# Transposes of q, k and the attention output on the DMA crossbar in place of TensorE

## The chip, the cores and the metric

The kernel runs on one core of one Trainium2 chip. The metric is the device time of one execution in microseconds; several runs are taken, and their median counts. The kernel before has a median of 389.23 us over 3 runs (389.01 to 389.64). Beside the timed runs there is one profiled execution, from which all views of the profile come.

## The reference

The work is a causal attention with a forget gate, followed by a two-layer network with an exact GELU. There are 8 batches of 8 heads, 576 tokens and 64 dimensions a head; the network sees 4608 tokens of 512 values, 2048 in the middle.

```
scores = q @ k.T / sqrt(64) + (cum[q] - cum[k])      # cum = cumsum(log(clip(f, 1e-4, 1)))
scores = where(key > query, -1e9, scores)
attn   = softmax(scores) ; o = attn @ v              # per batch and head
x      = o, heads side by side                       # 4608 x 512
out    = gelu(x @ w_in) @ w_out                      # 4608 x 2048, 4608 x 512
```

Inputs and output are float32; the kernel multiplies in bfloat16.

## The kernel before, in words

All order is written out by hand: each engine runs its instructions in the order of the program text, and only data and buffers make it wait. SP issues loads of f and v and all stores, POOL the loads of q, k and the weights (they are cast to bfloat16 on the way).

**Attention of a batch.** Two heads make a pair, and a batch has four pairs. `scores(b, i, t)` makes the tile t (0 to 3) of key-by-query scores of pair i for both heads: 2 or 4 matmuls (L251) into one of two score buffers, an exp on ScalarE (L261), and a causal mask on POOL (L263). `attend(b, i, h, ms)` (L282) multiplies the masked exps by the weighted v, with a column for the row sums; `normalize` (L295, L296, VectorE) divides, which gives the pair's x tile of tokens by (head, dimension). The program attends to a pair while the next pair's scores are made.

**The transposes.** The scores need q and k with the 64 dimensions on partitions: `qA[i]` holds the first head of the pair in the upper half and zeros in the lower, `qB[i]` the reverse, `kT[i]` both heads of k. q and k arrive as tiles of 96 partitions, six tokens in each. `transposes_pe(b, i)` transposes pair i with twelve TensorE transposes against an identity (L209); each takes two neighbouring tokens' 64 dimensions, so that even tokens lie in the upper and odd ones in the lower 64 partitions, and eight VectorE copies (L221) put them in their columns. The network needs x with features on partitions: `to_xT(b, i)` makes five transposes (L306) and one VectorE copy (L309) into `xT_sb`.

**The network.** A chunk is 512 tokens. `gemm1(c, ffb)` makes one of 16 blocks of the middle layer: four matmuls (L318), one for each pair's features, and a GELU on ScalarE (L330). `gemm2(c)` is a generator that gives one matmul (L350) at a time, 64 in a chunk; every sixteenth ends an output tile, which VectorE copies (L359) and SP stores (L360). Both use the two buffers of `m_psum`.

**How they interleave.** Batch 0 has a routine of its own, and its transposes stay as they are. For each later batch b, `attention(b, ...)` runs the attention, and after each `scores` call takes some matmuls from `gemm2(b - 1)`; the table FILL (FILL_1 for batch 1) says how many: a row for each pair, a column for each tile, and a last row for the places behind the last pair's scores. Then come the 16 blocks of `gemm1(b)`, and between them the transposes of the next batch's q and k, and POOL's weighing of its v. The first matmul of a block needs x of pair 0, the last x of pair 3. After batch 7 the remaining chunk follows without attention.

Of the kernel before, what the change touches and what calls it, by code (L numbers as in the profile page):

```python
# [9 lines left out]
BF16 = mybir.dt.bfloat16  # L10
# [4 lines left out]
P = 128  # L15
S = 576
D = 64
H = 8
HP = 4
# [3 lines left out]
JT = 6  # L23
PT = 96
# [25 lines left out]
def kernel(  # L50
# [10 lines left out]
    nc = tc.nc  # L61
    B = q.shape[0]
# [13 lines left out]
    qk_pool = ctx.enter_context(tc.tile_pool(name="qk", bufs=1))  # L76
    v_pool = ctx.enter_context(tc.tile_pool(name="v", bufs=1))
    e_pool = ctx.enter_context(tc.tile_pool(name="e", bufs=3))
    x_pool = ctx.enter_context(tc.tile_pool(name="x", bufs=3))
    g_pool = ctx.enter_context(tc.tile_pool(name="g", bufs=2))  # L80
    o_pool = ctx.enter_context(tc.tile_pool(name="outs", bufs=4))
# [5 lines left out]
    qk_of, v_of = {}, {}  # L87

    def load_qk_tokens(b, h0=0, h1=H):

        if b not in qk_of:
            qk_of[b] = [
                qk_pool.tile([PT, H, JT * D], BF16, tag=n, name=f"{n}{b}")
                for n in "qk"
            ]
        for src, dst in zip((q, k), qk_of[b]):
            nc.gpsimd.dma_start(  # L97
                dst[:, h0:h1, :],
                src[b, h0:h1].rearrange("h (p j) d -> p h (j d)", j=JT),
            )  # L100
# [28 lines left out]
    qA = [consts.tile([P, S], BF16, name=f"qA{i}") for i in range(HP)]  # L129
    qB = [consts.tile([P, S], BF16, name=f"qB{i}") for i in range(HP)]  # L130
    kT = [consts.tile([P, S], BF16, name=f"kT{i}") for i in range(HP)]
# [14 lines left out]
    def load_w_out():  # L146
        for kt in range(0, n_ff, 4):
            nc.gpsimd.dma_start(w_out_sb[:, kt : kt + 4, :], w_out_r[:, kt : kt + 4, :])
# [16 lines left out]
    xT_sb = consts.tile([P, n_dm, N_tok], BF16)  # L165
# [27 lines left out]
    def transposes_pe(b, i, in_s=True):  # L193

        shape = [P, 2, JT // 2, PT]
        if in_s:
            both = s_psum.tile([P, 2, 2 * 512], BF16, tag="s", name="s_t")
            pss = [
                both[:, w, 0:S].rearrange("p (h j t) -> p h j t", h=2, j=JT // 2)
                for w in range(2)  # L200
            ]
        else:
            pss = [
                o_psum.tile(shape, BF16, tag="o", name="ps_t") for _ in range(2)
            ]
        for src, ps in zip(qk_of[b], pss):
            for h in range(2):
                for j in range(JT // 2):
                    nc.tensor.transpose(  # L209
                        ps[:, h, j, :],  # L210
                        src[:, 2 * i + h, 2 * j * D : 2 * (j + 1) * D],
                        ident_bf[:PT, :PT],
                    )
        for which, ps in enumerate(pss):
            for h in range(2):
                dst = (qA[i], qB[i])[h] if which == 0 else kT[i]
                rows = dst[h * D : (h + 1) * D, :].rearrange(
                    "d (p j two) -> d two p j", j=JT // 2, two=2
                )
                for odd in range(2):  # L220
                    nc.vector.tensor_copy(  # L221
                        rows[:, odd],
                        ps[odd * D : (odd + 1) * D, h].rearrange("d j p -> d p j"),
                    )

    vw_of = {}

    def weigh_v(b, i, eng=None):
# [17 lines left out]
    def scores(b, i, t):  # L246
        st = s_psum.tile([P, 2, 512], FP32, tag="s", name=f"s{t}")
        c = 0
        for n, q0, w in STILES[t]:
            for h, qt in enumerate((qA[i], qB[i])):  # L250
                nc.tensor.matmul(  # L251
                    st[:, h, c : c + w],
                    kT[i][:, K0[n] : K0[n] + P],
                    qt[:, q0 : q0 + w],
                    start=True,
                    stop=True,
                )
            c += w
        et = e_pool.tile([P, 2, 512], BF16, tag=f"e{t}", name=f"e{t}")
        e_of[b, i, t] = et  # L260
        nc.scalar.activation(et[:, :, 0:c], st[:, :, 0:c], Act.Exp, scale=scale)  # L261
        for c0 in SDIAG[t]:
            nc.gpsimd.affine_select(  # L263
                out=et[:, :, c0 : c0 + P],
                in_=et[:, :, c0 : c0 + P],
                compare_op=Alu.is_ge,
                fill=0.0,
                base=0,
                pattern=[[0, 2], [1, P]],
                channel_multiplier=-1,  # L270
            )

    o_of, x_of = {}, {}

    def attend(b, i, h, ms):
        if (b, i, h) not in o_of:
            o_of[b, i, h] = o_psum.tile([P, NBLK, D + 1], FP32, tag="o", name="o")
        o = o_of[b, i, h]
        for m in ms:
            for n in range(m + 1):  # L280
                t, c = where(n, m)
                nc.tensor.matmul(  # L282
                    o[:, m, :],
                    e_of[b, i, t][:, h, c : c + P],
                    vw_of[b][:, 2 * i + h, n, :],
                    start=(n == 0),
                    stop=(n == m),
                )

    def normalize(b, i, h):  # L290
        if (b, i) not in x_of:
            x_of[b, i] = x_pool.tile([P, NBLK, 2, D], BF16, tag="x", name="x")
        o = o_of[b, i, h]
        r = x_pool.tile([P, NBLK], FP32, tag="r", name="r")
        nc.vector.reciprocal(r, o[:, :, D])  # L295
        nc.vector.tensor_tensor(  # L296
            x_of[b, i][:, :, h, :],
            o[:, :, 0:D],
            r.unsqueeze(2).to_broadcast([P, NBLK, D]),
            Alu.mult,  # L300
        )

    def to_xT(b, i, pool=o_psum, tag="o"):
        ps = pool.tile([P, S], BF16, tag=tag, name="ps_x")
        for m in (4, 3, 2, 1, 0):
            nc.tensor.transpose(  # L306
                ps[:, K0[m] : K0[m] + P], x_of[b, i][:, m, :, :], ident_bf
            )
        nc.vector.tensor_copy(xT_sb[:, i, b * S : (b + 1) * S], ps)  # L309


    g_of = {}
# [50 lines left out]
    def take(gen, n):  # L363
        for _ in range(n):
            if next(gen, "end") == "end":
                return


    def first_attention():
# [37 lines left out]
        scores(0, 2, 3)  # L407
        weigh_v(0, 3)
        to_xT(0, 0, m_psum, "m")
        scores(0, 3, 0)  # L410
        scores(0, 3, 1)
# [10 lines left out]

    FILL = [[5, 7, 4, 4], [2, 3, 3, 2], [2, 3, 3, 2], [2, 2, 2, 2], [8, 4, 4, 0]]
    FILL_1 = [[0, 0, 0, 0], [2, 2, 2, 2], [2, 2, 2, 2], [2, 2, 2, 2], [8, 4, 4, 0]]

    def attention(b, fill, counts):
        for i in range(HP):
            for t in range(4):  # L430
                scores(b, i, t)
                if i >= 2 and t == 0:
                    to_xT(b, i - 2)
                if i and t == 1:
                    attend(b, i - 1, 0, (0, 1, 2))
                elif i and t == 2:
                    attend(b, i - 1, 0, (3, 4))
                    normalize(b, i - 1, 0)
                elif i and t == 3:
                    attend(b, i - 1, 1, (0, 1, 2, 3, 4))  # L440
                    normalize(b, i - 1, 1)
                if b == 1 and i == 0 and t == 2:
                    transposes_pe(1, 3, in_s=False)
                    load_qk_tokens(2)
                take(fill, counts[i][t])
        i = HP - 1
        take(fill, counts[HP][0])
        attend(b, i, 0, (0, 1, 2, 3, 4))
        normalize(b, i, 0)
        to_xT(b, i - 1)  # L450
        take(fill, counts[HP][1])
        attend(b, i, 1, (0, 1, 2, 3, 4))
        normalize(b, i, 1)
        take(fill, counts[HP][2])
        to_xT(b, i)
        take(fill, 999)

    for b in range(B):
        if b == 0:
            first_attention()  # L460
            load_v(1, 0, 4)
            load_v(1, 4, 8)
        else:
            load_v(b + 1)
            attention(b, gemm2(b - 1, b == 1), FILL_1 if b == 1 else FILL)
        for ffb in range(n_ff):
            gemm1(b, ffb)
            if b + 1 < B:
                at = (10, 13, 15) if b == 0 else (0, 4, 8, 11)
                if ffb in at:  # L470
                    transposes_pe(b + 1, at.index(ffb))
                if ffb % 4 == 2:
                    weigh_v(b + 1, ffb // 4)
                if b == 0 and ffb == 2:
                    load_w_out()
        if 0 < b < B - 2:
            load_qk_tokens(b + 2)
# [35 lines left out]
```

## Time and profile before

| | |
|---|---|
| median of 3 runs | 389.23 us (389.01 to 389.64) |
| profiled execution | 389.12 us |
| its span, first to last instruction | 387.2 us |
| mean granted TensorE clock | 0.991 |
| TensorE matmuls busy | 363.6 us, 94% of the span |
| VectorE busy | 204.0 us, 53% |
| ScalarE busy | 217.8 us, 56% |
| GpSimd busy | 130.9 us, 34% |
| moved by DMA | 34.18 MB, mean 88 GB/s |

In the profile's rows PE is TensorE's matmuls, PEld its weight loads, DVE VectorE, ACT ScalarE, POOL GpSimd and SP SyncE; SPq is SP's queue of issues. L12 is line 12 of the kernel. A row of a group ends with its count, busy time, mean duration in ns, and the idle time of the engine before it with what ended that. A row of the chain of waits has a start, a length and what ran. Matmuls are pipelined and their ends are modelled, so a busy TensorE need not be at its peak; the chain counts each piece of its time once.

### The profile page before, as it was taken

To read this page: it belongs to the slowest core of one execution; us is meant where nothing else is said; L and a number is where in the kernel's file an instruction comes from. 1 tells how busy PE (TensorE), PEld (TensorE's weight loads), DVE (VectorE), ACT (ScalarE), POOL (GpSimd) and SP (SyncE) were. 2 spreads that over 40 slices of the span, in tenths; PEclk is the share of its full clock that TensorE was granted. 3 is DMA by queue.
4 is the path that set the end of the run, shared out by engine and by line. 5 is a ranking of instruction groups with operands and counts; after the bars stand their busy time and mean duration, and the time that the engine had idled before them with its cause. 6 is when DMAs were issued, how large, how long until landed. Compare 5 with 4: busy or idle time off the path is not lost.

```text
span 387.2 us, 7532 instructions
## 1 busy us (share of the span) xinstructions
PE 363.6 (94%) x3040; PEld 205.7 (53%) x3093; DVE 204.0 (53%) x448; ACT 217.8 (56%) x293; POOL 130.9 (34%) x261
## 2 busy tenths in 40 slices
PE   2889949999999999999999999999999999999996
PEld 1555536645565546654665556555655465444442
DVE  6483585549346953587358925693469545002011
ACT  4665656425873677457764678358736774621610
POOL 6675715341245134332425144513450242000000
PEclk9999978999999999999999999999999999999999
DMA  7999999145801781068213850188010010002002
GB/s 106 188 195 181 215 208 137 56 111 83 147 29 56 138 122 56 30 139 125 59 47 91 125 99 29 61 138 143 30 54 2 15 42 30 25 29 81 0 29 81
DMA packets 63954, 34.18 MB, mean 88 GB/s; under 512 B 42864, under 2 KB 59248, under 8 KB 63920
## 3 DMA queue, kind: packets, MB, share of 16 engines
q0 software_dynamic: 16896, 13.63, 23.7%
q1 hardware_dynamic: 47024, 20.08, 20.7%
q8 instruction: 24, 0.39, 0.4%
q14 instruction: 10, 0.08, 0.1%
HBM read 37.90 MB, written 9.44 MB: 122 GB/s over the span
## 4 chain that ended last, share of the span: by engine, by line
PE 90%; DVE 5%; ACT 2%; issue 1%; DMA 1%; ACTq 0%
PE ps L350 32%; PE ps L318 31%; PE s L251 13%; PE o L282 7%; PE s_t L209 3%; PE ps_x L306 2%; DVE ot L359 1%; ACT e L261 1%; PE ps_f L174 1%; DVE x L296 1%; DVE xT_sb L309 1%; DMA f_sb<-in_f_dram 1%; DVE kT L221 0%; DVE cum L161 0%; ACT L261 0%
## 5 line engine op out<-in xcount | busy, mean ns | idle before, releaser
L330 ACT ACTIVATE g<-ps 128x512 bf16<-128x512 f32 x144 | 86.0, 597 | 107.7 <-PE ps L318 107.7
L350 PE MATMUL ps<-w_out_sb,g 128*128 128x512 bf16 x540 | 138.9, 380 | 1.7
L318 PE MATMUL ps<-xT_sb,w_in_sb 128*128 128x512 bf16 x559 | 130.0, 379 | 1.5
L261 ACT ACTIVATE e<-s 128x1024 bf16<-128x1024 f32 (+2 forms) x128 | 107.3, 863 | 38.2 <-PE s L251 33.8
L263 POOL TENSOR_SCALAR_AFFINE_SELECT e<-e 128x256 bf16<-128x256 bf16 x160 | 63.8, 413 | 116.6 <-ACT e L261 115.6
L318 PEld LDWEIGHTS <-w_in_sb 128*128 128x128 bf16 x576 | 54.5, 98 | 60.8 <-issue 0.8
L350 PEld LDWEIGHTS <-g 128*128 128x128 bf16 x576 | 50.2, 98 | 40.0
L359 DVE COPY ot<-ps 128x512 f32<-128x512 f32 x36 | 24.8, 690 | 76.5 <-PE ps L350 72.9
L251 PE MATMUL s<-qA,kT 128*128 128x384 bf16 (+2 forms) x192 | 55.9, 299 | 8.5 <-ACT e L261 4.3
L251 PEld LDWEIGHTS <-kT 128*128 128x128 bf16 x384 | 37.7, 102 | 45.5 <-issue 8.2
L221 DVE COPY kT<-s_t 64x288 bf16<-64x288 bf16 x108 | 51.8, 480 | 1.5
L251 PE MATMUL s<-qB,kT 128*128 128x384 bf16 (+2 forms) x192 | 51.5, 300 | 0.3 <-DVE qB L182 0.3
L236 POOL TENSOR_TENSOR vw<-v,wT 128x640 bf16<-128x640 f32 x30 | 38.4, 1280 | 27.0 <-PE o L282 22.3
L295 DVE RECIPROCAL r<-o 128x5 f32<-128x5 f32 x64 | 12.4, 194 | 63.4 <-PE o L282 63.4
L282 PEld LDWEIGHTS <-e 128*128 128x128 bf16 x960 | 40.6, 98 | 8.1 <-DVE x L296 1.3
L282 PE MATMUL o<-vw,e 128*128 128x65 bf16 x960 | 43.9, 194 | 0.1
L221 DVE COPY qA<-s_t 64x288 bf16<-64x288 bf16 x54 | 25.9, 479 | 16.3 <-PE s_t L209 15.3
L296 DVE TENSOR_TENSOR x<-o,r 128x320 bf16<-128x320 f32 x64 | 31.5, 492 | 2.2
L221 DVE COPY qB<-s_t 64x288 bf16<-64x288 bf16 x54 | 25.9, 480 | 0.7
L97 POOL DMA_DIRECT2D q<-in_q_dram x12 | 9.1, 756 | 47.7 <-PE s_t L209 46.5
L309 DVE COPY xT_sb<-ps_x 128x576 bf16<-128x576 bf16 x32 | 14.5, 452 | 8.4 <-PE ps_x L306 8.4
L306 PE MATMUL ps_x<-ident_bf,x 128*128 128x128 bf16 x160 | 14.4, 220 | 2.1 <-DVE x L296 2.1
(49 smaller groups left out, 134.9 us busy)
## 6 DMA issues: line engine op xcount, KB each, us to landing
out_dram<-ot SPq DMA_DIRECT2D x36, 256.0 KB, 2.0
v<-in_v_dram SPq DMA_DIRECT2D x30, 256.0 KB, 4.7
q<-in_q_dram POOLq DMA_DIRECT2D x6, 576.0 KB, 6.3
k<-in_k_dram POOLq DMA_DIRECT2D x6, 576.0 KB, 8.3
v<-in_v_dram SPq DMA_DIRECT2D x20, 128.0 KB, 6.8
w_in_sb<-in_moe_w_in_dram POOLq DMA_DIRECT2D x4, 512.0 KB, 10.3
w_out_sb<-in_moe_w_out_dram POOLq DMA_DIRECT2D x4, 512.0 KB, 10.6
q<-in_q_dram POOLq DMA_DIRECT2D x4, 144.0 KB, 4.2
```

What stands on the lines that cost most here:

```text
L221: nc.vector.tensor_copy(rows[:, odd], ps[odd * D : (odd + 1) * D, h].rearrange("d j p -> d p j"),)
L236: eng.tensor_tensor(vw_of[b][:, hs, :, 0:D], v_of[b][:, hs, :, :], w.unsqueeze(3).to_broadcast([P, 2, NBLK, D]), Alu.mult,)
L251: nc.tensor.matmul(st[:, h, c : c + w], kT[i][:, K0[n] : K0[n] + P], qt[:, q0 : q0 + w], start=True, stop=True,)
L261: nc.scalar.activation(et[:, :, 0:c], st[:, :, 0:c], Act.Exp, scale=scale)
L263: nc.gpsimd.affine_select(out=et[:, :, c0 : c0 + P], in_=et[:, :, c0 : c0 + P], compare_op=Alu.is_ge, fill=0.0, base=0, pattern=[[0, 2], [ ...
L282: nc.tensor.matmul(o[:, m, :], e_of[b, i, t][:, h, c : c + P], vw_of[b][:, 2 * i + h, n, :], start=(n == 0), stop=(n == m),)
L296: nc.vector.tensor_tensor(x_of[b, i][:, :, h, :], o[:, :, 0:D], r.unsqueeze(2).to_broadcast([P, NBLK, D]), Alu.mult,)
L306: nc.tensor.transpose(ps[:, K0[m] : K0[m] + P], x_of[b, i][:, m, :, :], ident_bf)
L318: nc.tensor.matmul(ps, w_in_sb[:, kt, ffb * P : (ffb + 1) * P], xT_sb[:, kt, t0 : t0 + TC], start=(kt == 0), stop=(kt == n_dm - 1),)
L330: nc.scalar.activation(g_of[c][ffb], ps, Act.Gelu)
L350: nc.tensor.matmul(pss[ts], g_of[c][kt][:, ts * P : (ts + 1) * P], w_out_sb[:, kt, :], start=(kt == 0), stop=(kt == n_ff - 1),)
L359: nc.vector.tensor_copy(ot, pss[ts])
```

## The change

`transpose_dma(b, i)` has SP issue two transposing DMAs, one for q and one for k of a pair, from the loaded tile into new tiles `tq` and `tk`. They do what the TensorE transposes did, so even and odd tokens lie in the two halves, and `untangle(b, i)` makes the same eight VectorE copies, from SBUF instead of PSUM. `x_dma(b, i)` replaces `to_xT`: two transposing DMAs write straight into `xT_sb`, one for 512 tokens and one for the last 64. Batch 0 is as it was, and so are the transposes of batch 1's q and k. The DMAs of batch b+1's q and k are issued in the attention of batch b, the copies stand in `gemm1(b)`, and FILL and FILL_1 are new.

```diff
+    tq_pool = ctx.enter_context(tc.tile_pool(name="tq", bufs=1))
...
+    def transpose_dma(b, i):
+
+        if b not in tq_of:
+            tq_of[b] = [
+                tq_pool.tile([P, H, JT // 2, PT], BF16, tag="t" + n, name=f"t{n}{b}")
+                for n in "qk"
+            ]
+        hs = slice(2 * i, 2 * i + 2)
+        for src, dst in zip(qk_of[b], tq_of[b]):
+            nc.sync.dma_start_transpose(
+                dst[:, hs].rearrange("d h j p -> d (h j) p"),
+                src[:, hs].rearrange("p h c -> p (h c)"),
+            )
+
+    def untangle(b, i):
+
+        for which, src in enumerate(tq_of[b]):
+            for h in range(2):
+                dst = (qA[i], qB[i])[h] if which == 0 else kT[i]
+                rows = dst[h * D : (h + 1) * D, :].rearrange(
+                    "d (p j two) -> d two p j", j=JT // 2, two=2
+                )
+                for odd in range(2):
+                    nc.vector.tensor_copy(
+                        rows[:, odd],
+                        src[odd * D : (odd + 1) * D, 2 * i + h].rearrange(
+                            "d j p -> d p j"
+                        ),
+                    )
...
+    def x_dma(b, i):
+        x, q0 = x_of[b, i], b * S
+        nc.sync.dma_start_transpose(
+            xT_sb[:, i, q0 : q0 + 512].rearrange("d (m p) -> d m p", p=P),
+            x[:, 0:4].rearrange("p m h d -> p (m h d)"),
+        )
+        nc.sync.dma_start_transpose(
+            xT_sb[:, i, q0 + 512 : q0 + S].unsqueeze(1),
+            x[D:P, 4].rearrange("p h d -> p (h d)"),
+        )
...
-    FILL = [[5, 7, 4, 4], [2, 3, 3, 2], [2, 3, 3, 2], [2, 2, 2, 2], [8, 4, 4, 0]]
-    FILL_1 = [[0, 0, 0, 0], [2, 2, 2, 2], [2, 2, 2, 2], [2, 2, 2, 2], [8, 4, 4, 0]]
+    FILL = [[4, 6, 2, 2], [2, 2, 2, 2], [2, 2, 2, 2], [2, 2, 1, 1], [8, 4, 16]]
+    FILL_1 = [[0, 0, 0, 0], [2, 2, 2, 2], [2, 2, 2, 2], [2, 2, 2, 2], [8, 4, 99]]
...
-                if i >= 2 and t == 0:
-                    to_xT(b, i - 2)
...
                     attend(b, i - 1, 1, (0, 1, 2, 3, 4))
                     normalize(b, i - 1, 1)
+                    x_dma(b, i - 1)
...
+                if b + 1 < B:
+                    if b > 1 and t == 0 and i == 0:
+                        transpose_dma(b + 1, 0)
+                        transpose_dma(b + 1, 1)
+                    elif b > 1 and t == 0 and i in (1, 2):
+                        transpose_dma(b + 1, i + 1)
+                    elif b == 1 and (i, t) in ((2, 1), (3, 0), (3, 3)):
+                        transpose_dma(2, i + t // 2 - 2)
...
         take(fill, counts[HP][0])
         attend(b, i, 0, (0, 1, 2, 3, 4))
         normalize(b, i, 0)
-        to_xT(b, i - 1)
         take(fill, counts[HP][1])
         attend(b, i, 1, (0, 1, 2, 3, 4))
         normalize(b, i, 1)
-        take(fill, counts[HP][2])
-        to_xT(b, i)
+        x_dma(b, i)
+        if b == 1:
+            transpose_dma(2, 3)
         take(fill, 999)
...
-                at = (10, 13, 15) if b == 0 else (0, 4, 8, 11)
-                if ffb in at:
-                    transposes_pe(b + 1, at.index(ffb))
+                if b == 0 and ffb in (10, 13, 15):
+                    transposes_pe(b + 1, (10, 13, 15).index(ffb))
+                elif b and ffb % 4 == 0:
+                    untangle(b + 1, ffb // 4)
```

The line numbers move: in the changed kernel L238 issues the transposes of q and k, L252 is the copy of `untangle`, L346 and L350 issue the two of x, L328 and L329 normalize, L362 is the matmul of `gemm1`, L394 that of `gemm2`, L403 the output copy and L404 its store.

Two places show how instructions move. The first is VectorE at the end of the attention of batch 2, where the last pair's x is made (`x`, from the sums in `o`), an output tile is copied (`ot`) and the next batch's q and k follow. Before:

```order
L359 COPY ot<-ps_1588 128x512
L295 RECIPROCAL r<-o 128x5
L296 TENSOR_TENSOR x<-o,r 128x5x64
L309 COPY xT_sb<-ps_x 128x576
L295 RECIPROCAL r<-o 128x5
L296 TENSOR_TENSOR x<-o,r 128x5x64
L359 COPY ot<-ps_1729 128x512
L309 COPY xT_sb<-ps_x 128x576
L221 COPY qA_121<-s_t 64x288 x2
```

Now:

```order
L328 RECIPROCAL r<-o 128x5
L329 TENSOR_TENSOR x<-o,r 128x5x64
L403 COPY ot<-ps_1604 128x512
L328 RECIPROCAL r<-o 128x5
L329 TENSOR_TENSOR x<-o,r 128x5x64
L403 COPY ot<-ps_1713 128x512
L252 COPY qA_124<-tq_1372 64x288 x2
L252 COPY qB_128<-tq_1372 64x288 x2
```

The copies to xT_sb are gone, the third output tile's copy now stands between the two heads of the last pair, and the first copy of the next batch reads `tq` instead of PSUM.

The second place is SP's queue in the attention of batches 3 and 4. Before, it holds only v's loads and the stores:

```order
L360 DMA out_dram<-ot 128x512 x4
L108 DMA v_2011<-in_v_dram 128x8x64 x5
L360 DMA out_dram<-ot 128x512 x4
L108 DMA v_2606<-in_v_dram 128x8x64 x5
L360 DMA out_dram<-ot 128x512 x4
```

Now, from the first output store of an attention to the first transpose of its last pair's x:

```order
L404 DMA out_dram<-ot 128x512
L346 DMA_TRANSPOSE xT_sb<-x 128x4x128
L350 DMA_TRANSPOSE xT_sb<-x 128x1x64
L238 DMA_TRANSPOSE tq_2438<-q_2419 128x6x96
L238 DMA_TRANSPOSE tk_2439<-k_2420 128x6x96
L346 DMA_TRANSPOSE xT_sb<-x 128x4x128
L350 DMA_TRANSPOSE xT_sb<-x 128x1x64
L404 DMA out_dram<-ot 128x512
L346 DMA_TRANSPOSE xT_sb<-x 128x4x128
L350 DMA_TRANSPOSE xT_sb<-x 128x1x64
L404 DMA out_dram<-ot 128x512
L346 DMA_TRANSPOSE xT_sb<-x 128x4x128
```

The transposes of x, of the next batch's q and k, and the stores now stand in one queue, and one that waits for its data holds those behind it; the transposes of the last pair's x come just behind the third store.

More of the change, by code (lines that the diff above doesn't have):

```diff
@@ L224, in transposes_pe @@
                     )
+    tq_of = {}
+    def transpose_dma(b, i):
[24 more added lines that the diff above has]
+                    )
     vw_of = {}
```

## Prediction

> **What bounds the kernel now.** I read three views first: the table of stretches cut at one batch's period, the chain of waits over the last of these periods, and the groups by line.
>
> ```profile
> core 0: us, PE busy (x) PEld busy (x) DVE busy (x) ACT busy (x) POOL busy (x), PEclk, DMA share, GB/s
> 221.10:262.08 40.98, 40.52 (x359) 23.41 (x364) 25.15 (x57) 25.62 (x34) 15.13 (x30) 1.00 0.44 88
> 262.08:303.05 40.97, 40.51 (x360) 23.40 (x365) 25.14 (x57) 25.62 (x34) 13.53 (x28) 1.00 0.23 51
> by line: PE ps L350 33.1%; PE ps L318 32.8%; PE s L251 14.5%; PE o L282 9.2%; PE s_t L209 5.0%; PE ps_x L306 2.6%; DVE ot L359 1.7%; issue 1.1%; DVE xT_sb L309 0.9%
> ```
>
> Each batch from 2 to 6 takes 40.97 us (the five stretches differ by 0.1), TensorE is busy for 40.5 of them at full granted clock, VectorE and ScalarE for some 25. The chain over the last period is TensorE for 97%. So TensorE sets the pace, and what leaves it is worth its place in the chain. The transposes there are L209 (5.0%) and L306 (2.6%). Where attention ends and the first matrix product begins, the chain leaves TensorE:
>
> ```profile
> 283.57 0.47 PE o L282 x15
> 284.04 0.28 PE ps_x L306 x5
> 285.18 0.47 PE o L282 x15
> 285.66 0.88 PE ps L350 x4
> 286.53 0.02 issue
> 286.56 0.69 DVE ot L359
> 287.25 0.37 DVE xT_sb L309
> 287.67 0.38 PE ps L318
> 292.01 0.51 PE s_t L209 x12
> 272.86 0.40 PE ps_x L306 x5
> ```
>
> Here L306 of the last head pair is done soon after 286.53, but its copy L309 stands behind the output copy L359 on VectorE, and the last of four matmuls of L318 waits until 287.67.
>
> **What leaves TensorE.** q and k: one pair's twelve transposes take 0.51 us of the chain (row 292.01). They go from the first matrix product of batches 1 to 6, four pairs each: 24 x 0.51 = 12.2 us. The attention output: pairs 0 and 1 of a batch cost 0.40 (row 272.86), pair 2 0.28 (row 284.04). Batches 1 to 7 lose these: 7 x 1.08 = 7.6. At the end of batches 2 to 7, 286.53 to 287.67 is 1.14 us, in which three matmuls of L318 (0.22 each, 0.65) are useful: 0.49 x 6 = 2.9. In batch 1 the last pair's transposes have sixteen matmuls behind them, so there only their 0.28 goes. Together 23.0 us.
>
> **What the thinner filling costs.** The table FILL gives the attention loop 36 matmuls of L350 instead of 48. Where TensorE then comes early, it waits for ScalarE, since the scores have two buffers. I walk the first head pair along these rows:
>
> ```profile
> 262.08 0.44 PE s L251 x4
> 262.52 1.08 PE ps L350 x5
> 263.60 0.47 PE s L251 x2
> 262.73 1.28 ACT L261 ACT_TABLE_LOAD   x1
> 264.03 1.83 ACT L261 ACTIVATE e<-s 128x1024 bf16<-128x1024 f32 x2
> L261 ACT ACTIVATE e<-s 128x1024 bf16<-128x1024 f32 x64 | 65.5, 1024 | 33.0 <-PE s L251 29.4 <-POOL e L263 1.2 <-PE ps_x L306 1.1
> L261 ACT ACTIVATE e<-s 128x384 bf16<-128x384 f32 x32 | 15.6, 488 | 1.5 <-PE s L251 0.6
> L261 ACT ACTIVATE e<-s 128x896 bf16<-128x896 f32 x32 | 29.2, 914 | 3.7 <-PE s L251 3.7
> ```
>
> Let T be the start of the first scores (262.08 here). ScalarE's first two exps end at about T+3.0 and T+3.8, behind the table load. With 4 and 6 matmuls of 0.216 between, the third scores would start at T+2.9 and the fourth, two matmuls later, at T+3.9: waits under 0.1 each. The fifth would start at T+4.6 and needs the third exp, done a further 1.02 after T+3.9, so it waits about 0.4; the sixth and seventh find theirs done. From there a pair takes TensorE 1.43 of scores, 0.95 of attention and 6 to 8 matmuls, 3.7 to 4.1 us, against 1.02+0.91+1.02+0.49 = 3.45 of exps. Sum 0.55 per batch, six batches (batch 1 has an empty first row in both tables): 3.3 us. Bounds: 0, if the exps run a little earlier, and 1.1, if each pair waits once more; 0 to 6.6 in all.
>
> **What the moved transposes cost.** The trace has no crossbar transpose; every bound is from ordinary rows.
>
> ```profile
> out_dram<-ot SPq DMA_DIRECT2D x36, 256.0 KB, 2.0
> v<-in_v_dram SPq DMA_DIRECT2D x30, 256.0 KB, 4.7
> f_sb<-in_f_dram SPq DMA_DIRECT2D x1, 144.0 KB, 2.6
> q1 hardware_dynamic: 47024, 20.08, 20.7%
> 285.69 0.20 DVE L295 RECIPROCAL r<-o 128x5 f32<-128x5 f32 x1 [0.53 <-PE o L282]
> 285.92 0.49 DVE L296 TENSOR_TENSOR x<-o,r 128x320 bf16<-128x320 f32 x1
> ```
>
> Only one landing is near the path: x_dma of the last pair. Call A the end of that pair's second attention (285.66). Before, x is ready at A+0.75 (286.41). In the new order the third output tile ends with the fill just before this attention, so its 0.69 copy stands ahead on VectorE: it starts when the fill ends, 0.47 before A, and ends at about A+0.25; 0.20 and 0.49 behind it, x is ready at about A+1.0. TensorE has work until A + 16 x 0.216 + 0.65 = A+4.1. So a landing of up to 3.1 us is hidden, and each us beyond costs six batches 6 us (batch 1 has 28 matmuls there). Low bound: the output row, 2.0 from issue to landing. High bound: 128x512 elements read as 512 runs of 256 B but written as strips of sixteen 2-byte elements are 4096 pieces, 256 per DMA engine; a packet of this queue costs 0.207 x 16 x 387.2 / 47024 = 27 ns, so 6.9 us, plus the output row's 2.0 less its own data (128 rows, 8 an engine, 0.2): 8.7. I take 3.35, midway between the output row and v, because the 512 runs are half of one v transfer (1024 runs of 256 B, five queued together), and the queue is nearly idle there. It overruns by 0.25: 1.5 us.
>
> A page of the Trainium skill prices this otherwise: DMA: Bandwidth & Descriptors, section Latency and other measured facts, gives crossbar transposes an effective 261 GB/s. By it 128 KB would move in an estimated 0.5 us, the landing would be near the output row's, and the last 1.5 us would drop out of the sum. No run here shows it yet.
>
> The q and k transposes are issued at the head of the attention before and read in the next first product, over 20 us later (the like stretch ran from 262.08 to 286.53). Their sources come earlier too: POOL's loads, which waited 46.5 us in all for L209, now wait only for earlier transposes.
>
> ```profile
> POOL q L97 <- PE s_t L209: 46.5, 5, 13.3
> L221 DVE COPY kT<-s_t 64x288 bf16<-64x288 bf16 x108 | 51.8, 480 | 1.5
> L134 DVE MEMSET qA<- 64x288 uint32 x4 | 1.2, 298 | 0.4
> L242 DVE CAST vw<-wT 128x10 bf16<-128x10 f32 x2 | 0.6, 300 | 0.0
> ```
>
> SP holds later issues behind each waiting one: x_dma of an early pair or an output store may come some us late, and the four output buffers and three x buffers cover that. The copies that untangle keep their count, 32 a batch, and read SBUF. Bounds: 0.30 (the memset of that size) and 0.56 (0.30 for a nearly empty SBUF cast plus 288 elements at the 0.9 ns by which 64x288 and 64x576 copies differ, 0.48 to 0.74); I take 0.48, unchanged. They take 9.6 to 17.9 us beside 13.8 us of product (64 x 0.216), the first pair's 8 are done in 4.5 at most, and pair 3 is due 12 us into attention: 0 at either end.
>
> ```profile
> L182 DVE COPY kT<-ps_f 128x576 bf16<-128x576 bf16 x4 | 3.0, 740 | 6.3 <-PE ps_f L174 6.3
> ```
>
> **Sum.** 23.0 - 3.3 - 1.5 = 18.2 us. 387.2 - 18.2 = 369.0 of span; the profiled execution took 389.12, that is 1.92 more than its span, so 370.9; it lies 0.11 below the median of 389.23, so I say 371.0.
>
> **Rivals.**
> - *The landing is 4 to 6.3 us.* For: v's 4.7, and one transfer writes 128 partitions in small pieces. Against: nothing else is queued. At 4.7 the wait is 1.6 x 6 = 9.6, 379.1; the gain of 19.7 without landing waits is used up at 3.1 + 19.7/6 = 6.4 us.
>
> ```profile
> 250.22 4.09 SPq L108 DMA_DIRECT2D v<-in_v_dram  x5
> ```
>
> - *The crossbar is the bound (slower).* All transposes share SP's queue: eight of q or k with 96x768 elements (4608 strips, 288 per engine), four of 128x512 (256) and four of 64x128 (32) are 3456 strips an engine and batch. If strips cost p ns one after the other, that is 3.456 x p us. It passes the old period of 40.97 at p = 11.9 ns; at half of the 27 ns packet, 46.7 us a batch: 6 x 5.7 = 34 us slower, 423; at the whole of it, 93 us, some 700. For: no row shows strips cheaper. Against: the same queue issues five v transfers over 4.09 us and lands each in 4.7, so plain transfers of 256 KB overlap, and strips may be merged.
>  The Trainium skill has a price that points this way: VectorE: DVE Perf Modes, section The three transpose paths, gives 1309 ns for a 128x128 transpose by the crossbar. Laid end to end the 66 blocks of a batch would be an estimated 86 us, and the time near 660; the page does not say that they are serial, and nothing here shows it.
> - *ScalarE takes the gain.* If the exps hold the loop at every pair, with 2 us a batch instead of 0.55, it costs 8.7 more: 379.7. For: table load plus exps are 15.1 us, and TensorE's new loop (6.1 of scores, 2.9 of attention, 35 x 0.216) is only 16.5. Against: the walk above.
>
> **Chances.** Forecast 0.55 (landing 2 to 4 us, exps 0 to 1.1 a batch: 366 to 378); long landing 0.17 (378 to 391); crossbar bound 0.21 (above 391); ScalarE 0.07 (378 to 384). Faster takes the forecast, ScalarE and most of the long landings, 0.77; within 0.2% (0.8 us, about what this measurement can tell from none) 0.02; slower 0.21. For 8 in 10 the range is 366 to 391.
>
> **What would show it.** Right: a period near 37.8 us in the table of stretches, no transposes on TensorE after those of batch 1's q and k, the landing of the 128x4x128 transpose at 2 to 4 us in the list of DMA issues, and the wait of L362 for xT_sb under 0.5 us a batch. Wrong: L362 or L251 waiting for a DMA or for L252 by microseconds, transposes whose landings grow along a batch (the queue is the bound), or scores that wait for the exps at every pair.

## The result, and the profile after

The changed kernel takes 375.83 us (median of 4, 375.37 to 377.94) against 389.44 for the kernel before: a ratio of 0.966, 95% interval 0.962 to 0.970, 13.6 us faster. The forecast was 371.0 with a range of 366 to 391: the sign and the mechanism of the gain are right, and 4.8 us of the gain are missing. The profiled execution took 375.81 us, its span is 374.1. Below, a ratio leaves out executions over 1.5% slower than the fastest of their kernel.

The table of stretches of the changed kernel, cut at the last GELU ahead of each attention (the columns are those of the first row):

```profile
core 0: us, PE busy (x) PEld busy (x) DVE busy (x) ACT busy (x) POOL busy (x), PEclk, DMA share, GB/s
98.13:139.06 40.93, 37.72 (x298) 20.40 (x297) 19.92 (x52) 25.00 (x34) 15.15 (x30) 1.00 0.92 158
139.06:176.74 37.68, 37.49 (x298) 20.38 (x297) 19.93 (x52) 25.00 (x35) 15.15 (x30) 1.00 0.71 135
176.74:214.99 38.25, 37.57 (x298) 20.37 (x297) 19.91 (x52) 25.01 (x35) 15.15 (x30) 1.00 0.74 139
214.99:253.53 38.54, 37.56 (x298) 20.39 (x297) 19.91 (x52) 25.00 (x35) 15.14 (x30) 1.00 0.77 140
253.53:291.20 37.67, 37.48 (x298) 20.39 (x297) 19.51 (x52) 25.11 (x34) 13.63 (x28) 1.00 0.41 85
```

The period was 40.97 in every batch. Now two batches of these five take 37.67, the others 0.6, 0.9 and 3.3 us more, with nearly the same busy time on TensorE (37.5 to 37.7): it waits. The table of waits and the list of DMA issues say for what, and SP's queue, by line, how long one issue takes (min/median/max in ns):

```profile
PE ps L362 <- DMA xT_sb<-x: 7.9, 5, 3.6
xT_sb<-x SPq DMA_TRANSPOSE x56, 2.4
tq<-q SPq DMA_TRANSPOSE x24, 2.8
L346 SPq DMA_TRANSPOSE xT_sb<-x x28: 1194/1225/1599, 62.8 to 312.7; - x28
L350 SPq DMA_TRANSPOSE xT_sb<-x x28: 1212/1221/2277, 64.2 to 314.0; - x28
L238 SPq DMA_TRANSPOSE tq<-q x24: 1257/1273/2327, 65.5 to 265.4; - x24
```

At the median the transposes of x land in 2.4 us and those of q in 2.8, which the sixteen matmuls were to cover. But an issue occupies SP for 1.22 us, and the small one of 64 tokens (L350) as long as the one of 512 (L346). Sixteen a batch are 20 us of a queue that runs in order. The timeline at the end of batch 2's attention shows what follows:

```profile
114.16 2.55 SPq L238 DMA_TRANSPOSE tk<-k  x1
116.81 1.21 SPq L346 DMA_TRANSPOSE xT_sb<-x  x1
118.06 1.23 SPq L350 DMA_TRANSPOSE xT_sb<-x  x1
118.81 0.49 DVE L329 TENSOR_TENSOR x<-o,r 128x320 bf16<-128x320 f32 x1
119.39 0.52 SPq L404 DMA_DIRECT2D out_dram<-ot  x1
120.01 1.22 SPq L346 DMA_TRANSPOSE xT_sb<-x  x1
121.29 1.22 SPq L350 DMA_TRANSPOSE xT_sb<-x  x1
122.60 0.53 SPq L404 DMA_DIRECT2D out_dram<-ot  x1
123.22 1.22 SPq L346 DMA_TRANSPOSE xT_sb<-x  x1
125.70 0.81 PE L362 MATMUL ps<-xT_sb,w_in_sb 128*128 128x512 bf16 x3 [2.79 <-DMA xT_sb<-x]
```

The last pair's x is ready at 119.30 (118.81 + 0.49), but two transposes and two stores stand ahead of its own, which is issued at 123.22 and lands 2.4 later. In batch 1, x was ready at 75.15 (74.66 + 0.49) and issued at 82.13, behind four transposes and two stores:

```profile
74.66 0.49 DVE L329 TENSOR_TENSOR x<-o,r 128x320 bf16<-128x320 f32 x1
82.13 1.22 SPq L346 DMA_TRANSPOSE xT_sb<-x  x1
```

Sixteen issues alone do not make TensorE wait: batches 3 and 6 have as many and wait for no x. The queue has a second long occupant, the five loads of v behind each attention:

```profile
88.44 11.91 SPq L109 DMA_DIRECT2D v<-in_v_dram  x5
100.46 1.78 SPq L238 DMA_TRANSPOSE tq<-q  x1
196.16 2.28 SPq L350 DMA_TRANSPOSE xT_sb<-x  x1
```

They held SP for some 4 to 5 us a batch before (4.09 in the prediction's row) and hold it for 10.4 to 12.4 us now. Before, POOL's loads of q and k mostly began some 8.5 us behind them (217.71 behind 209.25); now both begin within 2.4 us (202.78 and 202.64 in batch 4). Batch 2's attention began at 98.1, so its first transpose of q, at 100.46, was already late; in batch 3 that issue came at 137.09, 2 us ahead of the attention. With the stores the queue is taken for some 33 of 37.7 us (20 + 11 + 2, an estimate from these rows). The short waits of batches 4 and 5, 0.5 and 0.8 us, each stand behind one issue of L350 that took 2.28 (row 196.16) or 2.15 us instead of 1.22.

### The profile page after: what moved, and what is told of

Same layout as the page of the kernel before. It is cut to its first block, busy times and chain, and to the rows that moved or that the text cites. A ratio compares the mean times of both kernels' runs of the same rounds, so it can differ in the third digit from the quotient of the medians.

```text
span 374.1 us, 6875 instructions
## 1 busy us (share of the span) xinstructions
PE 342.8 (92%) x2665; PEld 185.4 (50%) x2665; DVE 171.5 (46%) x420; ACT 214.0 (57%) x293; POOL 131.1 (35%) x261
## 3 DMA queue, kind: packets, MB, share of 16 engines
q1 hardware_dynamic: 94128, 31.30, 40.7%
## 4 chain that ended last, share of the span: by engine, by line
PE 77%; ACT 8%; DVE 7%; DMA 3%; SPq 2%; issue 1%; DVEq 0%; ACTq 0%
PE ps L362 33%; PE ps L394 26%; PE s L284 10%; PE o L315 7%; ACT e L294 5%; DMA xT_sb<-x 3%; ACT L294 2%; DVE vw L269 1%; ACT g L374 1%; SPq L350 1%; DVE x L329 1%; DVE ot L403 1%; DMA f_sb<-in_f_dram 1%; SPq L404 1%; DVE qB L183 1%
## 5 line engine op out<-in xcount | busy, mean ns | idle before, releaser
L394 PE MATMUL ps<-w_out_sb,g 128*128 128x512 bf16 x576 | 144.7, 379 | 0.0
L362 PE MATMUL ps<-xT_sb,w_in_sb 128*128 128x512 bf16 x576 | 127.2, 379 | 7.9 <-DMA xT_sb<-x 7.9
L294 ACT ACTIVATE e<-s 128x1024 bf16<-128x1024 f32 (+2 forms) x128 | 103.5, 861 | 25.5 <-PE s L284 24.9
L296 POOL TENSOR_SCALAR_AFFINE_SELECT e<-e 128x256 bf16<-128x256 bf16 x160 | 62.5, 407 | 140.0 <-ACT e L294 138.8
L362 PEld LDWEIGHTS <-w_in_sb 128*128 128x128 bf16 x576 | 56.1, 98 | 76.5 <-issue 10.3
L403 DVE COPY ot<-ps 128x512 f32<-128x512 f32 x36 | 24.9, 692 | 125.7 <-PE ps L394 124.8
L394 PEld LDWEIGHTS <-g 128*128 128x128 bf16 x576 | 50.3, 98 | 41.0
L284 PE MATMUL s<-qA,kT 128*128 128x384 bf16 (+2 forms) x192 | 54.8, 293 | 9.6 <-ACT e L294 4.2
L284 PE MATMUL s<-qB,kT 128*128 128x384 bf16 (+2 forms) x192 | 50.3, 294 | 0.3 <-DVE qB L183 0.3
L328 DVE RECIPROCAL r<-o 128x5 f32<-128x5 f32 x64 | 12.4, 193 | 48.0 <-PE o L315 47.1
L252 DVE COPY kT<-tk 64x288 bf16<-64x288 bf16 x96 | 32.2, 336 | 1.4
L329 DVE TENSOR_TENSOR x<-o,r 128x320 bf16<-128x320 f32 x64 | 31.5, 492 | 2.2
L252 DVE COPY qA<-tq 64x288 bf16<-64x288 bf16 x48 | 20.8, 433 | 0.9
L252 DVE COPY qB<-tq 64x288 bf16<-64x288 bf16 x48 | 16.7, 348 | 0.7
## 6 DMA issues: line engine op xcount, KB each, us to landing
w_in_sb<-in_moe_w_in_dram POOLq DMA_DIRECT2D x4, 512.0 KB, 10.2
w_out_sb<-in_moe_w_out_dram POOLq DMA_DIRECT2D x4, 512.0 KB, 13.6
```

What stands on the lines that cost most here:

```text
L252: nc.vector.tensor_copy(rows[:, odd], src[odd * D : (odd + 1) * D, 2 * i + h].rearrange("d j p -> d p j"),)
L284: nc.tensor.matmul(st[:, h, c : c + w], kT[i][:, K0[n] : K0[n] + P], qt[:, q0 : q0 + w], start=True, stop=True,)
L296: nc.gpsimd.affine_select(out=et[:, :, c0 : c0 + P], in_=et[:, :, c0 : c0 + P], compare_op=Alu.is_ge, fill=0.0, base=0, pattern=[[0, 2], [ ...
L329: nc.vector.tensor_tensor(x_of[b, i][:, :, h, :], o[:, :, 0:D], r.unsqueeze(2).to_broadcast([P, NBLK, D]), Alu.mult,)
L362: nc.tensor.matmul(ps, w_in_sb[:, kt, ffb * P : (ffb + 1) * P], xT_sb[:, kt, t0 : t0 + TC], start=(kt == 0), stop=(kt == n_dm - 1),)
L394: nc.tensor.matmul(pss[ts], g_of[c][kt][:, ts * P : (ts + 1) * P], w_out_sb[:, kt, :], start=(kt == 0), stop=(kt == n_ff - 1),)
```

## The experiments

Theory A says that the missing time is SP's queue: issues of 1.22 us each, so the last x is late. A' gives the queue's time to the bytes or blocks of a transpose instead, and B says that landings are slow because other transfers share the DMA engines. Line numbers differ by a few between these kernels.

### Twice the issues, and a fourth of them

Splitting each transpose of q and k in two, by head:

```diff
-            nc.sync.dma_start_transpose(
-                dst[:, hs].rearrange("d h j p -> d (h j) p"),
-                src[:, hs].rearrange("p h c -> p (h c)"),
-            )
+            for h in range(2 * i, 2 * i + 2):
+                nc.sync.dma_start_transpose(dst[:, h], src[:, h])
```

> Each transpose of q and k is split in two, one head each: 16 issues a batch for 8, same bytes. Theory A: from the start of attention to the last x, SP issues 16 x 1.25 + 7 x 1.22 + 3 x 0.5 = 30 us against some 23 us of TensorE's work, so L362 waits 5 to 8 us in each of six or seven batches: span 400 to 420. Theory A' and B: no more than 2 us from 374.1.

433.65 us in one execution, span 431.9. The row of an issue, the waits, and the stretch of the first half of one first product in this kernel:

```profile
L239 SPq DMA_TRANSPOSE tq<-q x48: 1178/1247/2384, 65.2 to 320.5; - x48
PE ps L360 <- DMA xT_sb<-x: 51.3, 13, 9.4
132.67:157.50 24.83, 10.24 (x33) 3.74 (x33) 11.78 (x35) 4.18 (x7) 1.65 (x3) 0.59 1.06 171
```

Half the data, the same 1.25 us: the bytes are unchanged and the matmuls' waits went from 7.9 to 51.3 us. A' and B as whole explanations fall. The span lies beyond A's 420, and part of why is the granted clock: 0.59 in this stretch, behind long waits.

Merging them, one transpose for all eight heads of q and one for k, at the head of attention (in batch 1 at the place of pair 0):

```diff
-        hs = slice(2 * i, 2 * i + 2)
+        hs = slice(0, H)
...
                     if b > 1 and t == 0 and i == 0:
                         transpose_dma(b + 1, 0)
-                        transpose_dma(b + 1, 1)
-                    elif b > 1 and t == 0 and i in (1, 2):
-                        transpose_dma(b + 1, i + 1)
-                    elif b == 1 and (i, t) in ((2, 1), (3, 0), (3, 3)):
-                        transpose_dma(2, i + t // 2 - 2)
+                    elif b == 1 and (i, t) == (2, 1):
+                        transpose_dma(2, 0)
```

> The four transposes of q of a batch become one over all eight heads, and so do those of k; same bytes, 2 issues a batch for 8. Theory A (SP's queue: a transpose holds it about 1.22 us whatever its size, and the last pair's x comes late behind the others): the merged issue takes 1.3 to 1.6 us, L362 waits for xT_sb under 1 us in all instead of 7.9, span near 366.5, time near 368.3. Theory A' (the queue is held by the bytes or blocks, not by the instruction): the merged issue takes about 5.1 us, the wait stays near 7.9, time near 376. Theory B (the last x lands late because other transfers share the DMA engines): issues fall, but the wait stays at 5 us or more, time 373 to 376.

The ratio is 0.953 (0.947 to 0.958), but the four executions spread from 368.4 to 375.3 (median 373.54). Only the one of 375.18, span 373.2, has a profile; what the faster ones did is not shown. It has every period at 37.67 to 37.72 but batch 1's, and this one wait:

```profile
PE ps L362 <- DMA xT_sb<-x: 5.7, 1, 5.7
79.99 1.23 SPq L346 DMA_TRANSPOSE xT_sb<-x  x1
DMA to landing us min/median/max: 6.9/6.9/6.9
80.02 0.82 POOL L98 DMA_DIRECT2D q<-in_q_dram  x1
95.35 4.19 SPq L238 DMA_TRANSPOSE tq<-q  x1
99.65 2.93 SPq L238 DMA_TRANSPOSE tk<-k  x1
80.40:101.42 21.02, 15.25 (x64) 6.55 (x64) 11.29 (x33) 8.96 (x15) 1.20 (x2) 0.92 1.15 199
125.20:139.09 13.89, 13.84 (x64) 6.26 (x64) 12.45 (x33) 8.96 (x15) 4.12 (x6) 1.00 0.95 162
```

So A holds for batches 2 to 7. In batch 1 there is a place for B: the merged transposes free q's and k's tiles early, POOL loads batch 3's at 80.02 instead of 87.93, and that load meets the last x, which takes 6.9 us to land instead of 2.4. TensorE pays twice: behind the wait the same 64 matmuls run at a mean clock of 0.92, which makes the stretch 1.4 us longer than the wait explains (21.02 - 13.89 - 5.7). On the price of an issue theory A was wrong: it expected 1.3 to 1.6 us for a merged one, A' 5.1, and here q's take 3.8 to 5.4 and k's 2.8 to 3.7. 1.2 us is a floor up to the size of a pair; above it the size counts. At the medians (4.7 and 3.0) the merge takes only 2.5 of the 10.2 us a batch that eight issues of 1.27 hold, and it also moves all of them to the head of the attention; which of the two cleared batches 2 to 7 was not tested apart.

### The same issues in another order

The 64-token transposes of a batch go behind the last pair's 512-token one; x gets eight buffers:

```diff
-        nc.sync.dma_start_transpose(
-            xT_sb[:, i, q0 + 512 : q0 + S].unsqueeze(1),
-            x[D:P, 4].rearrange("p h d -> p (h d)"),
-        )
+        if i == HP - 1:
+            for j in range(HP):
+                nc.sync.dma_start_transpose(
+                    xT_sb[:, j, q0 + 512 : q0 + S].unsqueeze(1),
+                    x_of[b, j][D:P, 4].rearrange("p h d -> p (h d)"),
+                )
```

> The four 64-token transposes of a batch's x are issued together behind the last pair's 512-token one (x gets eight buffers for it); same issues, same bytes, another order. Theory A: three issues of 1.22 us leave the queue ahead of the last 512-token transpose, which is 3.7 us earlier: the wait of L362 falls from 7.9 to under 2 us, span 367 to 368.5, time near 369.5. Theory A': the 64-token ones hold little, the wait stays above 6 us. Theory B: the wait stays above 6 us, time near 375.

373.29 us (ratio 0.962, 0.957 to 0.968), span 371.6, where A expected 367 to 368.5. With no issue and no byte less, batch 1's wait falls from 3.6 to 1.2 and those of batches 4 and 5, 1.3 together, are gone, as A says and not A' or B. But batch 2 keeps 2.9 of its 3.0 us, because there SP stood for the loads:

```profile
PE ps L365 <- DMA xT_sb<-x: 4.1, 3, 1.6
89.81 12.22 SPq L110 DMA_DIRECT2D v<-in_v_dram  x5
109.87 1.28 SPq L239 DMA_TRANSPOSE tk<-k  x1
```

The five loads of v hold the queue until 102, and the transposes of the first three pairs' q and k end at 111, 16 us after this attention began at 95.4. Another 1.8 us went where TensorE's clock fell behind these waits (15.63 busy there against 13.85 in the next clean product; the row is in the last section).

### The collision in batch 1 alone

The merged kernel, with batch 3's loads held on POOL until a block of batch 1's first product is done:

```diff
         if 0 < b < B - 2:
+            if b == 1:
+                hold = consts.tile([P, 1], BF16, name="hold")
+                nc.gpsimd.tensor_copy(hold, g_of[1][3][:, 0:1])
             load_qk_tokens(b + 2)
```

> The kernel with merged transposes of q and k, and the loads of batch 3's q and k held on POOL until the fourth block of batch 1's first product is done, by one small copy; nothing else. There x of batch 1's last pair took 6.9 us to land beside these loads. Theory B for this place: issued near 80 again, it lands in 2.4 to 2.7, the first product waits 1.3 to 1.8 us for it instead of 5.9, TensorE keeps its full clock behind it, span near 367.5 in every run. If the landing was slow for another reason (the queue's own transposes and stores ahead of it), it stays over 5 us and the span near 373.

369.65 us (369.12 to 370.0; ratio 0.951, 0.950 to 0.952), span 368.1. The load now starts at 87.31, and x, issued at the same place of the program, lands in 2.4:

```profile
80.65 1.25 SPq L346 DMA_TRANSPOSE xT_sb<-x  x1
87.31 0.81 POOL L98 DMA_DIRECT2D q<-in_q_dram  x1 [0.33 <-issue]
DMA to landing us min/median/max: 2.4/2.4/2.4
PE ps L362 <- DMA xT_sb<-x: 2.3, 1, 2.3
84.85 10.40 SPq L109 DMA_DIRECT2D v<-in_v_dram  x5
84.36 4.57 SPq L109 DMA_DIRECT2D v<-in_v_dram  x5
```

The wait of 2.3 is more than the 1.3 to 1.8 expected because the issue came 0.66 later and the product began 0.35 earlier. It is the queue's share; the rest of the 5.7 was the collision. Without it four executions spread by 0.9 us instead of 6.9. The last two rows are v's loads without the hold (84.85, merged kernel) and with it (84.36): the same loads of q and k, when they run beside v's, also make v's hold SP for 10.4 us instead of 4.57.

### Both edits: the queue cleared

> Both edits together: one transpose for q and one for k a batch, and the 64-token transposes of x behind the last pair's 512-token one. Theory A (late issue on SP): x of the last pair is issued as soon as it is ready in every batch, every period is 37.67, no wait for xT_sb over 0.2 us, span 365.5 to 366.5, time near 367.8, and the runs spread by less than 1 us. Theory B (landing slowed by other transfers) has its place in batch 1 alone: with x issued near 76 us, 3.5 us before the loads of batch 3's q and k, that landing is 2.4 to 2.6 too. If B acts elsewhere, landings over 3 us stay in some batch.

368.41 us (367.4 to 368.88; ratio 0.947, 0.946 to 0.949), span 366.6, no wait for xT_sb in any batch:

```profile
94.86:132.53 37.67, 37.48 (x297) 20.40 (x296) 19.91 (x52) 25.00 (x34) 15.16 (x30) 1.00 0.68 130
132.53:170.21 37.68, 37.49 (x298) 20.40 (x297) 19.90 (x52) 25.01 (x34) 15.15 (x30) 1.00 0.75 143
```

Time and span are those of theory A, to 0.6 us. Executions spread by 1.5 us, not 1. Batch 1's last x was issued at 78.8, not 76, 1.8 us ahead of the loads, and landed in 2.6.

### Less cover for the last x

Both edits, with eight of the sixteen matmuls moved ahead of the last x:

```diff
-    FILL = [[4, 6, 2, 2], [2, 2, 2, 2], [2, 2, 2, 2], [2, 2, 1, 1], [8, 4, 16]]
+    FILL = [[4, 6, 2, 2], [2, 2, 2, 2], [2, 2, 2, 2], [2, 2, 1, 1], [16, 4, 8]]
```

> The kernel with both edits, and the last row of FILL [16, 4, 8] for [8, 4, 16]: eight of the sixteen matmuls behind the last pair's x go ahead of it. Theory A and the measured landing of 2.4: the cover becomes 8 x 0.216 + 0.65 - 0.75 = 1.6 us, with some 0.1 to start the issue each of six batches waits 0.8 to 1.0 us, span 5 to 6 us above the kernel with both edits. With the 3.35 of the prediction it would be 1.7 a batch, 10 us. If the landing were off the path, no difference.

374.43 us in one execution, span 372.6: 6.0 above. The period and the waits:

```profile
172.35:210.98 38.63, 37.56 (x297) 20.40 (x296) 21.48 (x52) 25.01 (x34) 15.25 (x30) 1.00 0.73 131
PE ps L365 <- DMA xT_sb<-x: 5.9, 6, 1.5
```

About 1.0 a batch: cover and landing add up as expected, with 2.4 for the landing and not 3.35.

### One half of the change at a time

Only q and k by the crossbar: the calls of `x_dma` give way to `to_xT` at its old places, the last one with twelve matmuls behind it.

```diff
+                if i >= 2 and t == 0:
+                    to_xT(b, i - 2)
...
-                    x_dma(b, i - 1)
...
         normalize(b, i, 0)
+        to_xT(b, i - 1)
...
-        x_dma(b, i)
         if b == 1:
             transpose_dma(2, 3)
+        take(fill, 4)
+        to_xT(b, i)
```

> Only q and k go by the crossbar; x is transposed by TensorE at its old places, the last pair's with twelve matmuls behind it. From the span of the changed kernel: minus 7.9 of waits for xT_sb, plus 7 x 1.36 = 9.5 of transposes, of which 1 to 2 us fill places where TensorE waits for ScalarE: span 374 to 375.7, time 376 to 377.5. If the x transposes on the crossbar were worth their whole 1.36 a batch and the waits came from something else, the waits would show at another line and the span would be 380 or more.

379.11 us in one execution, span 377.4. No wait for xT_sb, and the period is

```profile
135.08:174.36 39.28, 38.70 (x312) 21.45 (x317) 21.35 (x56) 25.23 (x34) 15.10 (x30) 1.00 0.62 122
```

that is 1.61 over the clean one, where 1.36 less some filled waits was expected; so the span is above the 374 to 375.7 expected. The transposes filled nothing; in the chain they take 0.40, 0.40, 0.28 and, for the last pair, 0.45, together 1.53. So x on the crossbar is worth all of it.

Only x by the crossbar: `transposes_pe` again for all batches, no `transpose_dma`, no `untangle`.

```diff
-                if b == 0 and ffb in (10, 13, 15):
-                    transposes_pe(b + 1, (10, 13, 15).index(ffb))
-                elif b and ffb % 4 == 0:
-                    untangle(b + 1, ffb // 4)
+                at = (10, 13, 15) if b == 0 else (0, 4, 8, 11)
+                if ffb in at:
+                    transposes_pe(b + 1, at.index(ffb))
```

> Only x goes by the crossbar; q and k of all batches are transposed by TensorE between the blocks of the first product, as before. Theory A: SP has eight transposes a batch, x is never late, no wait for xT_sb over 0.2 us in batches 2 to 7; the period is 37.67 + 4 x 0.51 = 39.7, span 366.2 + 24 x 0.51 = 378.4, time near 380. Theory B expects the same here, since q and k load at their old time. If the first product's clean time hides part of these transposes, less.

380.34 us in one execution, span 378.3, period

```profile
136.02:175.76 39.74, 39.46 (x345) 22.35 (x344) 23.50 (x53) 25.07 (x34) 15.02 (x30) 1.00 0.52 106
```

As forecast: four times 0.51 over the clean period, and with eight transposes a batch on SP the first product waits for no x.

### The wait for the exps

Both edits, and two matmuls moved from behind the last x into the first pair:

```diff
-    FILL = [[4, 6, 2, 2], [2, 2, 2, 2], [2, 2, 2, 2], [2, 2, 1, 1], [8, 4, 16]]
+    FILL = [[4, 7, 3, 2], [2, 2, 2, 2], [2, 2, 2, 2], [2, 2, 1, 1], [8, 4, 14]]
```

> The kernel with both edits, and FILL with a first row [4, 7, 3, 2] for [4, 6, 2, 2] and a last row [8, 4, 14] for [8, 4, 16]: two matmuls go from behind the last pair's x into the first pair, where TensorE waits 0.5 us a batch for the exps. If those 0.5 us are a pure wait on ScalarE, 0.43 a batch come back, six batches 2.6 us: span near 364.1, period 37.24, time near 365.8. The cover of the last x falls to 2.7 us, just over its landing of 2.4 and the start of the issue; if that is too little, the wait for xT_sb returns with up to 0.2 a batch. If the wait is set by something else (the score buffers with the later scores), no gain, or later exps.

365.94 us (365.19 to 366.43), ratio 0.941 (0.939 to 0.942): the fastest of all, ahead of both kernels of this case.

```profile
205.84:243.09 37.25, 36.93 (x292) 20.40 (x297) 20.24 (x52) 25.01 (x34) 15.15 (x30) 1.00 0.78 143
PE ps L365 <- DMA xT_sb<-x: 0.2, 1, 0.2
```

The period fell by 0.42, the two matmuls that fill the wait. The waits for xT_sb are 0.2 in all, so 14 matmuls still cover the landing.

## Why the prediction was right, and where its sum failed

- **What leaves TensorE, 23.0 us: right as far as measured.** The single halves show it: q and k on TensorE cost 39.74 - 37.67 = 2.07 a batch (4 x 0.51 = 2.04 predicted), x 39.28 - 37.67 = 1.61 (1.36 predicted for the transposes alone; the last pair's take 0.45 and not 0.28). The 0.49 at the end of a batch is not in this difference, since that half hides it too; no run measures it alone.
- **The thinner filling, 0.55 a batch: right in place and size.** In the kernel with both edits the first scores start at 132.53 and the fifth at 137.48, 4.95 later, with 4.45 of work between (scores 0.44, 0.38, 0.44, 0.17, fourteen matmuls of 0.216): 0.50. Filling it gave 0.42 back.
- **The landing, 3.35 us: too long.** 2.4, near the low bound. The high bound counted strips; the trace counts runs of 256 B. The queue's packets rise from 47024 to 94128 (row below), by 47,104: that is 43,776 runs of 256 B in the 104 transposes (28 x 512, 28 x 64 and 48 x 576) and 32 more for each transpose. So, as the trace counts, the landing on the path has 512 pieces of data and not 4096. By the Trainium skill's effective 261 GB/s for crossbar transposes (DMA: Bandwidth & Descriptors, Latency and other measured facts) the landing was estimated near the output row's, and the trace agrees: 2.4 beside 2.3. The Trainium skill's 1309 ns for one 128x128 transpose (VectorE: DVE Perf Modes, The three transpose paths) do not add up block after block: four such blocks land in 2.4 us.

```profile
q1 hardware_dynamic: 94128, 31.30, 40.7%
```

- **The failing step** is in the term for the moved transposes: "Only one landing is near the path: x_dma of the last pair", with its time counted from when x is ready, and of SP only that "x_dma of an early pair or an output store may come some us late, and the four output buffers and three x buffers cover that". I priced the landing and gave the issue no price, though the queue's issues were listed. That "the queue is nearly idle there" was read from the kernel before. In the changed one, issues of 1.22 us, the stores, and v's loads, which hold SP for 10 to 12 us, put the last x 3.9 us late in batch 2 and 7.0 in batch 1, where I had seen 28 matmuls of cover and no risk. That q and k would load earlier I had counted as help; that these loads would meet v's and slow SP's queue I had not seen. The term was 1.5 us and measured 7.9. With it the sum is 23.0 - 3.0 - 7.9 = 12.1; the spans differ by 13.1. The last 1.0 I can't place; the short gaps called issue, 1.1% of the period before, are where I would look.
- **Luck, and the signs.** The 1.5 us stood for a long landing, which did not come; with the landing right the term would have been 0 and the forecast 369.5. One error covered part of the other. Of the signs named ahead, the period (37.67) and the landing came out right. But L362 waited for a DMA by up to 3.6 us, which was named as a sign of being wrong, and rightly so for this term.
- **The copies that untangle, 0: right.** They take 0.33 us at the median (0.48 from PSUM before), and no wait of TensorE for them stands in the table. (The row read there as 64x576 is of 128x576; as the term is 0 at either bound, nothing hangs on it.)

```profile
L252 DVE COPY kT<-tk x96: 320/325/674, 82.4 to 289.5; 64x288 bf16<-64x288 bf16 x96
```

- **The rivals.** The crossbar as the bound has its place, SP's queue, but not its price: per issue and not per strip. Doubling the issues makes it true, 431.9 of span. Long landings occur, up to 6.6 us in the changed kernel, but TensorE waited for none of them there; in the merged kernel it waited for one of 6.9, beside a load. ScalarE did not hold every pair; its sum of 16.5 us has 6.1 for scores where four pairs at 1.43 are 5.7, and 35 matmuls for 36, which changes nothing.

## What to carry to other kernels

Price a moved step by what its issue holds as well as by its landing, and add up everything that stands ahead of the one on the path in its queue, loads and stores too; then merge issues, or order them by due time. A transfer that is made ready earlier also releases the next load earlier, and that load can land on the one transfer that is due: look for what the freed buffer triggers.

## What was not expected of the hardware

- A crossbar transpose from SBUF to SBUF occupies SP for 1.22 us at 64x128 and at 128x512, 1.27 at 96x768, and at 96x3072 for a median of 4.7 (q) and 3.0 (k) in the merged kernel, where a plain store takes 0.52. Some take longer, 16 of the 104 in the changed kernel from 1.57 up to 2.55 us (rows 114.16 and 196.16 are two). That cause stays open.
- Behind a wait of 5.7 us the stretch of 21 us had a mean clock of 0.92, and the loss lay in its first 3 us: 0.56 from 86.9 to 90.0, then 1.00. Behind 3.6 us in batch 1 of the changed kernel the clock stayed at 1.00, as its stretch shows. Two waits of 1.2 and 1.6 us with one matmul between them, in the kernel with the other order, gave 0.91. So a late transfer can cost more than its wait; where the limit lies was not measured.

```profile
80.36:97.93 17.57, 13.97 (x66) 6.25 (x65) 11.55 (x33) 8.96 (x15) 1.59 (x2) 1.00 0.87 167
119.22:137.77 18.55, 15.63 (x65) 6.54 (x65) 12.43 (x33) 8.96 (x15) 4.13 (x6) 0.91 1.19 196
```
